# Halved first products and a seeded last accumulation in a retention + two-MLP kernel

## The chip, the core and the metric

The kernel runs on one core of one Trainium2 chip. The metric is the device time of one execution in microseconds (us). Before the change it is 582.34 us, the median of two runs (582.31 and 582.37).

## What is computed

A retention layer (linear attention with a per-head decay, 2 batches of 8 heads, 768 positions of 64 channels) gives a matrix x of 1536 tokens by 512 channels. Two MLPs follow. Everything is in float32.

```python
h = x @ w_in                                        # first MLP: 512 -> 2048
g = np.maximum(h, 0.0) + alpha * np.minimum(h, 0.0)
x = g @ w_out                                       # 2048 -> 512
h = x @ w_in2                                       # second MLP
r = np.maximum(h, 0.0)
out = (r * r) @ w_out2
```

## The kernel before, in words

Retention comes first (up to line 538, about the first 54 us). The change touches only the second MLP, and there only its last part.

Both MLPs work on token tiles of 512 tokens (`TT`, three tiles t = 0, 1, 2) and on 16 blocks f of 128 hidden channels (`NF`). To keep float32 accuracy each operand is split into a high and a low part of type fp32r (`wh`, `wl`, `xh`, `xl`, `gh`, `gl`), and each product is three matmuls: low times high, high times low, high times high.

A **step** is one pair (t, f) of one MLP m. The list `STEPS` (line 47) has 96 of them, 48 for each MLP, in the order of `PARTS` (lines 34 to 38). A **part** is a run of blocks f of one token tile that is accumulated in PSUM without interruption. The second MLP's parts are tile 0 with f 0 to 7, tile 1 with f 0 to 7, tile 2 with all f, tile 1 with f 8 to 15, and last tile 0 with f 8 to 15. These last eight are the steps 88 to 95; tile 1's second part before them is steps 80 to 87.

For each step s the loop at line 553 does:

1. `first` (line 169): 12 matmuls of 512 columns into one PSUM bank (4 blocks of the 512 input channels, 3 matmuls each), line 176. The innermost loop takes the weights in the order wl, wh, wh.
2. `activate` (line 181): for the second MLP a Relu on ScalarE (line 185), the square as a multiplication on VectorE (line 186), and the rounding to `gh` on ScalarE (line 195).
3. `rest` (line 198): `gl` on VectorE (line 200).
4. `load_sums` (line 235), at the last step of a part that continues an earlier one: four DMAs of 256 KB, issued by SyncE (line 238), fetch the earlier part's sums from DRAM into four tiles `ps` of the pool `pp`.
5. `second` (line 203) of step s - 2 (`LAG` is 2): for each of four groups i, three matmuls of 512 columns into the accumulator `acc[t][i]` (lines 226 to 231; 12 in all, line 231 in the second MLP). The accumulators rotate over PSUM banks 3 to 7. In the last part, the products of f = 14 are held back and done together with those of f = 15, group by group.

At the end of a part `end_sum` (line 240) empties each accumulator. A first part is copied to a tile `p` by ScalarE (line 250) and written to DRAM as sums (line 252). A part that continues one is added to `ps` by VectorE (line 245), and the result goes to the output by a DMA on SyncE's queue (line 255).

Every engine runs its own instructions in the order in which the program issues them, and waits at an instruction for what that needs. SyncE's queue too: its DMAs start in the program's order. The pool `pp` (line 85) has four buffers for all `p` and `ps` tiles, so a new `ps` tile waits until the DMA has read the tile that had the buffer before:

```python
    pp = ctx.enter_context(tc.tile_pool(name="pp", bufs=4))
...
        p_of[t] = [pp.tile([128, 512], F32, tag="p", name=f"ps{m}_{t}_{i}") for i in range(4)]
        for i in range(4):
            nc.sync.dma_start(p_of[t][i], sums[m, t, i])
```

Of the kernel before, what the change touches and what calls it, by code (L numbers as in the profile page):

```python
# [21 lines left out]
NC = DM // 128  # L22
NF = DFF // 128
TT = 512
# [9 lines left out]
PARTS = [  # L34
    [(0, range(4)), (1, range(4)), (2, range(8)), (1, range(4, 8)), (0, range(4, 16)),
     (1, range(8, 16)), (2, range(8, 16))],
    [(0, range(8)), (1, range(8)), (2, range(16)), (1, range(8, 16)), (0, range(8, 16))],
]
LAG = 2
# [12 lines left out]
    if 0 <= i < len(STEPS)  # L52
]
SEQ = list(dict.fromkeys(USES))
BACC = dict(dynamic_dma_scratch_size=4096)


@with_exitstack
def retention_then_two_mlps(
# [15 lines left out]
    nc = tc.nc  # L75
# [17 lines left out]
    def bank(name, banks):  # L93

        i = used[banks] = used.get(banks, -1) + 1
        return psum["mlp"].tile([128, 512], F32, tag=f"bank{banks[i % len(banks)]}", name=name)
# [13 lines left out]
    def load_piece(queue=nc.scalar):  # L110
        if len(loaded) < 4 * NF:
            j = SEQ[len(loaded)]
            loaded.append(j)
# [4 lines left out]
    class Conversion:  # L118
# [3 lines left out]
        def start(self, k):  # L122
            if k < 4 * NF and SEQ[k] not in bits:
                j = SEQ[k]
                low, high = raws[j][:, :, 0], raws[j][:, :, 1]
                bits[j] = x = bitp.tile([128, DM], U32, tag="bits", name=f"bits{j}")
                nc.scalar.activation(x.bitcast(F32), high.bitcast(F32), AF.Copy, scale=REBIAS)  # L127
                nc.scalar.activation(low.bitcast(I32), low, AF.Copy, scale=2.0**-29)  # L128

        def begin(self):  # L130

            j = SEQ[self.k]
            x, high = bits[j], raws[j][:, :, 1]
# [5 lines left out]
        def middle(self, load=True):  # L139

            j = SEQ[self.k]
            x, low, slot = bits[j], raws.pop(j)[:, :, 0], j % (2 * NF)
# [7 lines left out]
        def end(self):  # L150
            j = SEQ[self.k]
            x, hi, slot = bits.pop(j).bitcast(F32), weights[j], j % (2 * NF)
            lo = wpools[slot // 2].tile([128, DM], F32R, tag=f"wl{slot}", name=f"wl{j}")
            nc.vector.tensor_tensor(lo, x, hi.bitcast(F32), ALU.subtract)  # L154
            weights[j] = hi, lo
            self.k += 1
# [7 lines left out]
    steps = STEPS  # L164
    x_of = {(0, t): xt[t] for t in range(NTILE)}
    g_of, acc = {}, {}
    sums = dram.tile([2, NTILE, 4, 128, TT], F32, name="sums")

    def first(m, t, f):
        wh, wl = weights[2 * (m * NF + f)]  # L170
        xh, xl = x_of[m, t]
        ph = bank(f"h{m}_{t}_{f}", (0, 1, 2))
        for c in range(NC):
            cols = slice(c * 128, (c + 1) * 128)
            for i, (w, x) in enumerate(((wl, xh), (wh, xl), (wh, xh))):
                nc.tensor.matmul(  # L176
                    ph, w[:, cols], x[:, c, :], start=c == 0 and i == 0, stop=c == NC - 1 and i == 2
                )
        return ph

    def activate(m, t, f, ph, on_act):
        g = tp.tile([128, TT], F32, tag="g", name=f"g{m}_{t}_{f}")
        a = alpha_sb[:, f : f + 1]
        if m == 1:
            nc.scalar.activation(g, ph, AF.Relu)  # L185
            nc.vector.scalar_tensor_tensor(g, ph, 0.0, g, ALU.max, ALU.mult)  # L186
        elif on_act:
            nc.scalar.activation(g, ph, AF.Relu, scale=-1.0)
            nc.scalar.activation(g, g, AF.Copy, scale=a)  # L189
            nc.vector.scalar_tensor_tensor(g, ph, 0.0, g, ALU.max, ALU.subtract)  # L190
        else:
            nc.vector.tensor_scalar(g, ph, 0.0, a, ALU.min, ALU.mult)
            nc.vector.scalar_tensor_tensor(g, ph, 0.0, g, ALU.max, ALU.add)
        gh = gp.tile([128, TT], F32R, tag="gh", name=f"gh{m}_{t}_{f}")
        nc.scalar.copy(gh, g)  # L195
        return g, gh

    def rest(m, t, f, g, gh):
        gl = gp.tile([128, TT], F32R, tag="gl", name=f"gl{m}_{t}_{f}")
        nc.vector.tensor_tensor(gl, g, gh.bitcast(F32), ALU.subtract)  # L200
        g_of[m, t, f] = gh, gl

    def second(m, t, f, part):
        if f == part[0]:
            acc[t] = [bank(f"acc{m}_{t}_{f}_{i}", (3, 4, 5, 6, 7)) for i in range(4)]

        last = m == 1 and (t, part) == PARTS[1][-1]
        if last and f == NF - 2:
            return
        fs = (NF - 2, NF - 1) if last and f == NF - 1 else (f,)  # L210
        for i in range(4):
            for e in fs:
                partial_sum(m, t, e, part, i)
            if f == part[-1]:
                end_sum(m, t, part, i)
        for e in fs:
            g_of.pop((m, t, e))
        if m == 0 and f == NF - 1:
            next_x(t, part)

    def partial_sum(m, t, f, part, i):
        wh, wl = weights[2 * (m * NF + f) + 1]
        gh, gl = g_of[m, t, f]
        cols = slice(i * 128, (i + 1) * 128)

        for j, (w, g) in enumerate(((wl, gh), (wh, gh), (wh, gl))):
            flags = dict(start=f == part[0] and j == 0, stop=f == part[-1] and j == 2)
            if m == 0:
                nc.tensor.matmul(acc[t][i], w[:, cols], g, **flags)  # L229
            else:  # L230
                nc.tensor.matmul(acc[t][i], g[:, cols], w, **flags)  # L231

    p_of = {}

    def load_sums(m, t):
# [4 lines that stand above are left out]
    def end_sum(m, t, part, i):  # L240

        done = part[-1] == NF - 1
        if part[0] > 0:
            p = p_of[t][i]
            nc.vector.tensor_tensor(p, acc[t][i], p, ALU.add)  # L245
        elif m == 0 and done:
            p = acc[t][i]
        else:
            p = pp.tile([128, 512], F32, tag="p", name=f"p{m}_{t}_{part[0]}_{i}")
            nc.scalar.copy(p, acc[t][i])  # L250
        if not done:
            nc.sync.dma_start(sums[m, t, i], p)
        elif m == 1:
            c, b = ORDER[t * CPT + i]
            nc.sync.dma_start(out[b * S + c * CH : b * S + (c + 1) * CH, :], p)
        else:
            acc[t][i] = p

    def next_x(t, part):
        xh, xl = x_of[1, t] = x_tile("xb", t)  # L260
        ps = acc.pop(t)
        for i in range(5):
            if i < 4:
                nc.scalar.copy(xh[:, i, :], ps[i])
            if i > 0:
                nc.vector.tensor_tensor(
                    xl[:, i - 1, :], ps[i - 1], xh.bitcast(F32)[:, i - 1, :], ALU.subtract
                )
# [51 lines left out]
    def where(name, shape, pattern, base, fill, channel=1):  # L320

        x = ap1.tile(shape, F32, name=name)
        zeros = warm[0 : shape[0], 0 : shape[-1]]
        if len(shape) == 3:
            zeros = zeros.unsqueeze(1).to_broadcast(shape)
        nc.gpsimd.affine_select(
            x, zeros, pattern=pattern, compare_op=ALU.not_equal, fill=fill, base=base,
            channel_multiplier=channel,
        )
        return x  # L330

    head = ap1.tile([H, NPAIR, 2, D], F32, name="head")
    for t in range(2):
        m = where(f"head{t}", [H, NPAIR, D], [[-2, NPAIR], [0, D]], -t, 1.0)
# [218 lines left out]
    for s in range(len(steps) + LAG):  # L553
        if s < len(steps):
            m, t, f, part = steps[s]
            sums_end = s >= LAG and steps[s - LAG][2] == steps[s - LAG][3][-1]
            unit = conv.k < 4 * NF and not sums_end
            if unit and SEQ[conv.k] >= 2 * NF and free[(SEQ[conv.k] - 2 * NF) // 2] >= s:
                unit = False
            if unit:  # L560
                conv.start(conv.k + 1)
                conv.begin()
            ph = first(m, t, f)
            g, gh = activate(m, t, f, ph, unit)
            if unit:
                conv.middle()
            rest(m, t, f, g, gh)
            if unit:
                conv.end()
            if f == part[-1] and part[0] > 0:  # L570
                load_sums(m, t)
        if s >= LAG:
            second(*steps[s - LAG])


# [58 lines left out]
```

## Time and profile before

| | us |
|---|---|
| time, median of 2 runs | 582.34 |
| the profiled execution | 582.9 |
| its span, first to last instruction | 580.6 |
| TensorE (PE) busy | 572.1 |
| weight loads (PEld) busy | 475.7 |
| VectorE (DVE) busy | 334.7 |
| ScalarE (ACT) busy | 293.6 |
| mean granted TensorE clock (1.0 is full) | 1.00 |

The profile is of one execution. Times in its rows are counted from the span's start. A matmul's duration in a row includes its way through the array and so overlaps with the next one's; the distance from start to start says how fast matmuls follow each other. "L176" is line 176. "SPq" is SyncE's queue of DMA issues, "PEld" the weight load that belongs to a matmul.

### The profile page before, as it was taken

What the parts mean: (1) busy time and instruction counts of PE and PEld (TensorE: products, weight loads), DVE (VectorE), ACT (ScalarE), POOL (GpSimd) and SP (SyncE); (2) the same over time, 40 slices, a digit from 0 to 9 for tenths busy, and PEclk for the clock granted to TensorE, in tenths of its full rate; (3) what the DMA queues carried; (4) which work ended last, traced back from release to release, by engine and by line L of the source; (5) the groups of instructions that cost most, each with busy time, mean ns of one, the idle gap of its engine ahead of it and who ended that gap; (6) DMA issues with size and microseconds to landing.
All of it is one profiled execution on the core that took longest, in us unless ns stands there. A gap on an engine that the chain in (4) does not pass through costs nothing.

```text
span 580.6 us, 7855 instructions
## 1 busy us (share of the span) xinstructions
PE 572.1 (99%) x3058; PEld 475.7 (82%) x3058; DVE 334.7 (58%) x535; ACT 293.6 (51%) x509; POOL 33.3 (6%) x34
## 2 busy tenths in 40 slices
PE   8998999999999999999999999999999999999997
PEld 7887888888888888888888888888888888888885
DVE  3888766666666666866866965665632222222422
ACT  2566765765746765765765654654522222322220
POOL 2785000000000000000000000000000000000000
PEclk9999999999999999999999999999999999999999
DMA  7993343323544223333333123423100000400401
GB/s 255 361 393 120 108 146 109 117 102 109 192 147 168 82 100 109 110 108 110 108 110 109 51 94 110 141 78 109 73 0 1 0 1 0 146 0 1 145 2 72
DMA packets 25732, 62.38 MB, mean 107 GB/s; under 512 B 2904, under 2 KB 3936, under 8 KB 25696
## 3 DMA queue, kind: packets, MB, share of 16 engines
q1 hardware_dynamic: 17488, 32.01, 15.7%
q10 hardware_dynamic: 8208, 29.89, 15.5%
q8 instruction: 24, 0.39, 0.3%
q14 instruction: 12, 0.10, 0.0%
HBM read 52.44 MB, written 9.45 MB: 107 GB/s over the span
## 4 chain that ended last, share of the span: by engine, by line
PE 95%; DMA 3%; DVE 1%; issue 0%; SPq 0%; DVEq 0%
PE h L176 45%; PE acc L231 22%; PE acc L229 22%; PE o L436 2%; PE o L444 2%; PE s L399 1%; DMA q<-in_qt_dram 1%; DMA r<-in_kr_dram 1%; DMA zd<-z 1%; PE pk L459 1%; DMA lam_sb<-in_lam_dram 0%; DVE err L358 0%; DVE ps L245 0%; SPq L304 0%; DVE low L359 0%
## 5 line engine op out<-in xcount | busy, mean ns | idle before, releaser
L195 ACT CAST gh<-g 128x512 fp32r<-128x512 f32 x96 | 59.6, 621 | 90.5 <-DVE g L186 37.5
L186 DVE SCALAR_TENSOR_TENSOR g<-h,g 128x512 f32<-128x512 f32 x48 | 33.2, 691 | 123.4 <-ACT g L185 123.4
L185 ACT ACTIVATE g<-h 128x512 f32<-128x512 f32 x48 | 28.7, 598 | 124.3 <-PE h L176 124.3
L200 DVE TENSOR_TENSOR gl<-g,gh 128x512 fp32r<-128x512 f32 x96 | 66.5, 692 | 30.3 <-ACT gh L195 21.6
L176 PE MATMUL h<-xah,wl 128*128 128x512 f32 x192 | 74.8, 390 | 0.0
L176 PE MATMUL h<-xah,wh 128*128 128x512 f32 x192 | 74.7, 389 | 0.0
L176 PE MATMUL h<-xal,wh 128*128 128x512 f32 x192 | 74.7, 389 | 0.0
L229 PE MATMUL acc<-gh,wl 128*128 128x512 f32 x192 | 74.7, 389 | 0.0
L229 PE MATMUL acc<-gh,wh 128*128 128x512 f32 x192 | 74.7, 389 | 0.0
L229 PE MATMUL acc<-gl,wh 128*128 128x512 f32 x192 | 74.7, 389 | 0.0
L176 PE MATMUL h<-xbh,wl 128*128 128x512 f32 x192 | 74.7, 389 | 0.0
L176 PE MATMUL h<-xbl,wh 128*128 128x512 f32 x192 | 74.7, 389 | 0.0
L176 PE MATMUL h<-xbh,wh 128*128 128x512 f32 x192 | 74.7, 389 | 0.0
L231 PE MATMUL acc<-wl,gh 128*128 128x512 f32 x192 | 74.7, 389 | 0.0
L231 PE MATMUL acc<-wh,gh 128*128 128x512 f32 x192 | 74.7, 389 | 0.0
L231 PE MATMUL acc<-wh,gl 128*128 128x512 f32 x192 | 74.7, 389 | 0.0
L190 DVE SCALAR_TENSOR_TENSOR g<-h,g 128x512 f32<-128x512 f32 x42 | 29.0, 691 | 62.2 <-ACT g L189 62.2
L135 DVE SCALAR_TENSOR_TENSOR bits<-raw,bits 128x512 uint32<-128x512 uint32 x64 | 46.9, 733 | 2.2
L154 DVE TENSOR_TENSOR wl<-bits,wh 128x512 fp32r<-128x512 f32 x64 | 44.6, 697 | 2.7 <-ACT wh L145 2.7
L143 DVE CUSTOM_DVE_ANT_0 bits<-raw,bits 128x1024 uint16<-128x1024 uint16 x64 | 46.0, 718 | 0.0
L127 ACT ACTIVATE bits<-raw 128x512 f32<-128x512 f32 x64 | 43.0, 672 | 0.7 <-DMA raw<-in_w_dram 0.6
L128 ACT ACTIVATE raw<-raw 128x512 int32<-128x512 uint32 x64 | 42.7, 667 | 0.0
(73 smaller groups left out, 786.4 us busy)
## 6 DMA issues: line engine op xcount, KB each, us to landing
raw<-in_w_dram ACTq DMA_DIRECT2D x57, 512.0 KB, 3.3
ps<-sums SPq DMA_DIRECT2D x24, 256.0 KB, 3.1
sums<-p SPq DMA_DIRECT2D x20, 256.0 KB, 2.2
raw<-in_w_dram SPq DMA_DIRECT2D x7, 512.0 KB, 6.3
k<-in_kt_dram SPq DMA_DIRECT2D x12, 256.0 KB, 5.9
q<-in_qt_dram SPq DMA_DIRECT2D x12, 256.0 KB, 5.3
v<-in_vr_dram SPq DMA_DIRECT2D x12, 256.0 KB, 6.0
r<-in_kr_dram SPq DMA_DIRECT2D x10, 256.0 KB, 5.7
```

The source lines that it names most:

```text
L127: nc.scalar.activation(x.bitcast(F32), high.bitcast(F32), AF.Copy, scale=REBIAS)
L128: nc.scalar.activation(low.bitcast(I32), low, AF.Copy, scale=2.0**-29)
L135: nc.vector.scalar_tensor_tensor(x, high, 0x80000000, x, ALU.bitwise_and, ALU.bitwise_or)
L143: nc.vector.tensor_tensor(x.bitcast(I32), x.bitcast(I32), low.bitcast(I32), ALU.add)
L154: nc.vector.tensor_tensor(lo, x, hi.bitcast(F32), ALU.subtract)
L176: nc.tensor.matmul(ph, w[:, cols], x[:, c, :], start=c == 0 and i == 0, stop=c == NC - 1 and i == 2)
L186: nc.vector.scalar_tensor_tensor(g, ph, 0.0, g, ALU.max, ALU.mult)
L190: nc.vector.scalar_tensor_tensor(g, ph, 0.0, g, ALU.max, ALU.subtract)
L195: nc.scalar.copy(gh, g)
L200: nc.vector.tensor_tensor(gl, g, gh.bitcast(F32), ALU.subtract)
L229: nc.tensor.matmul(acc[t][i], w[:, cols], g, **flags)
L231: nc.tensor.matmul(acc[t][i], g[:, cols], w, **flags)
```

## The change

Two edits. The first products of steps 88 to 91 (second MLP, tile 0, f 8 to 11) are issued as 24 matmuls of 256 columns in place of 12 of 512: each pair of halves has the same weights and writes the two halves of the same bank. And the last part (steps 88 to 95) is seeded: at its start ScalarE copies the four `ps` tiles into the four accumulators, the matmuls then add to them, and at the end the accumulator is copied to a tile `p` by ScalarE (line 250 of before) where VectorE had added `ps`. The loads of the sums for this part are issued in step 89, after `second` of step 87, where they were issued in step 95.

```diff
@@ -52,6 +52,7 @@
+HALVED = range(8, 12)
@@ -170,12 +171,17 @@ first
         ph = bank(f"h{m}_{t}_{f}", (0, 1, 2))
+        cut = TT // 2 if (m, t) == (1, 0) and f in HALVED else TT
+        halves = [slice(a, a + cut) for a in range(0, TT, cut)]
         for c in range(NC):
             cols = slice(c * 128, (c + 1) * 128)
             for i, (w, x) in enumerate(((wl, xh), (wh, xl), (wh, xh))):
-                nc.tensor.matmul(
-                    ph, w[:, cols], x[:, c, :], start=c == 0 and i == 0, stop=c == NC - 1 and i == 2
-                )
+                for ts in halves:
+                    nc.tensor.matmul(
+                        ph[:, ts], w[:, cols], x[:, c, ts],
+                        start=c == 0 and i == 0 and ts.start == 0,
+                        stop=c == NC - 1 and i == 2, skip_group_check=len(halves) > 1,
+                    )
         return ph
@@ -200,9 +206,15 @@
+    def seeded(m, t, part):
+        return m == 1 and (t, part) == PARTS[1][-1]
+
     def second(m, t, f, part):
         if f == part[0]:
             acc[t] = [bank(f"acc{m}_{t}_{f}_{i}", (3, 4, 5, 6, 7)) for i in range(4)]
+            if seeded(m, t, part):
+                for i in range(4):
+                    nc.scalar.copy(acc[t][i], p_of[t][i])
@@ -224,7 +236,10 @@ partial_sum
-            flags = dict(start=f == part[0] and j == 0, stop=f == part[-1] and j == 2)
+            flags = dict(
+                start=f == part[0] and j == 0 and not seeded(m, t, part),
+                stop=f == part[-1] and j == 2, skip_group_check=seeded(m, t, part),
+            )
@@ -240,7 +255,7 @@ end_sum
-        if part[0] > 0:
+        if part[0] > 0 and not seeded(m, t, part):
             p = p_of[t][i]
             nc.vector.tensor_tensor(p, acc[t][i], p, ALU.add)
@@ -567,10 +582,14 @@ main loop
-            if f == part[-1] and part[0] > 0:
+            if f == part[-1] and part[0] > 0 and not seeded(m, t, part):
                 load_sums(m, t)
         if s >= LAG:
             second(*steps[s - LAG])
+        if LAG <= s < len(steps) and seeded(*steps[s][:2], steps[s][3]):
+            m, t, f, part = steps[s]
+            if f == part[0] + 1:
+                load_sums(m, t)
```

## Rows read from the trace of the kernel before

**Rows 1.** The page: span, busy time of the engines, chain by engine.
```profile
span 580.6 us, 7855 instructions
PE 572.1 (99%) x3058; PEld 475.7 (82%) x3058; DVE 334.7 (58%) x535; ACT 293.6 (51%) x509; POOL 33.3 (6%) x34
PE 95%; DMA 3%; DVE 1%; issue 0%; SPq 0%; DVEq 0%
```
**Rows 2.** Chain that ended last, 530 to 581 us: start, us, what.
```profile
541.51 2.72 PE acc L231 x12
...
568.71 8.17 PE acc L231 x36
...
576.91 0.69 DVE ps L245
```
**Rows 3.** Timeline of PE, 538 to 545 us (start, duration): step 90.
```profile
538.63 0.39 PE L176 MATMUL h<-xbh,wl 128*128 128x512 f32 x1
538.86 0.39 PE L176 MATMUL h<-xbl,wh 128*128 128x512 f32 x1
...
541.35 0.39 PE L231 MATMUL acc<-wl,gh 128*128 128x512 f32 x1
...
544.07 0.39 PE L176 MATMUL h<-xbh,wl 128*128 128x512 f32 x1
```
**Rows 4.** Timeline of the other engines, 535 to 552 us (idle time before in brackets).
```profile
538.73 2.48 DVE L245 TENSOR_TENSOR ps<-acc,ps 128x512 f32<-128x512 f32 x4
539.44 2.13 SPq L255 DMA_DIRECT2D out_dram<-ps  x4
541.55 0.60 ACT L185 ACTIVATE g<-h 128x512 f32<-128x512 f32 x1 [3.46 <-PE h L176]
541.66 2.51 SPq L238 DMA_DIRECT2D ps<-sums  x4
542.90 0.62 ACT L195 CAST gh<-g 128x512 fp32r<-128x512 f32 x1 [0.76 <-DVE g L186]
```
**Rows 5.** Line 238 in 533 to 549 us: issues, and time to landing.
```profile
L238 SPq DMA_DIRECT2D ps<-sums x4: 319/333/404, 541.7 to 543.9; - x4
DMA to landing us min/median/max: 3.0/3.2/3.4
```
**Rows 6.** DMA traffic, 539 to 548 us in 40 slices of 0.225 us.
```profile
GB/s 0 0 0 0 0 91 400 364 392 401 364 382 382 373 401 355 382 218 164 137 264 400 364 382 364 373 246 282 273 346 337 237 228 182 127 100 9 0 0 0
```
**Rows 7.** Groups by line and form: busy us, mean ns, idle before.
```profile
L176 PEld LDWEIGHTS h<-xbh,wh 128*128 128x128 f32 x192 | 36.1, 188 | 7.4
L176 PEld LDWEIGHTS h<-xbl,wh 128*128 128x128 f32 x192 | 36.0, 188 | 7.6
L436 PE MATMUL o<-sc,v 128*64 128x128 f32 x192 | 13.1, 279 | 1.9 <-issue 1.6 <-PE o L436 0.3
L250 ACT COPY p<-acc 128x512 f32<-128x512 f32 x24 | 12.2, 595 | 0.0
```
**Rows 8.** Timelines of PE and PEld, 13 to 15.2 us: the second warm-up.
```profile
13.08 2.05 PE L318 MATMUL warm_ps<-warm 128*128 128x128 f32 x16
...
13.08 1.86 PEld L318 LDWEIGHTS warm_ps<-warm 128*128 128x128 f32 x16
```
**Rows 9.** Line 318, durations min/median/max, and PE's timeline; a stretch (PE busy, clock, DMA).
```profile
L318 PE MATMUL warm_ps<-warm x40: 275/275/580, 1.0 to 14.9; 128*128 128x128 f32 x40
...
0.99 4.45 PE L318 MATMUL warm_ps<-warm 128*128 128x128 f32 x24 [0.99 <-POOL warm L313]
...
0.90:1.50 0.60, 0.51 (x2) 1.00 0.00 0
```
**Rows 10.** PE's timeline, 44 to 62 us; the stretch 46 to 52 us.
```profile
50.25 1.09 PE L436 MATMUL o<-sc,v 128*64 128x128 f32 x16 [1.58 <-issue]
...
46.00:52.00 6.00, 4.42 (x79) 1.00 0.30 95
```
**Rows 11.** Line 245, durations min/median/max, all 24.
```profile
L245 DVE TENSOR_TENSOR ps<-acc,ps x24: 681/681/692, 169.0 to 576.9; 128x512 f32<-128x512 f32 x24
```

## The prediction

> **What bounds the kernel now.** I read the page first: TensorE is busy for 572.1 of 580.6 us, and the chain that ended last lies on it for 95% [rows 1]. The chain in order of time then shows where this holds around the change: products follow products, 2.72 us for every twelve, without a gap, until the last product, one VectorE addition and the output DMA [rows 2]. So in the steps concerned each microsecond in which TensorE stands still is a microsecond of the time, and other engines' work is worth nothing except after the last product. The timeline of TensorE gives the unit: twelve first products start from 538.63 to 541.35, so one matmul of 512 columns takes 0.227 us from start to start, and a group of three 0.68 us [rows 3]. These are step 90's, and the products from 541.35 to 544.07 are `second` of step 88: the first that would need a seed. The timeline of the other engines shows where the sums are then [rows 4]: their loads are issued only at 541.66 us, after TensorE has begun those products. Before, nothing needs them until the end of the part, 30 us later.
>
> **Halves.** Four steps issue 24 matmuls for 12, and 24 weight loads for 12: `first` uses wh twice in a row already, and each of these has its own load (192 loads with xbl and 192 with xbh, 188 ns each) [rows 7], so equal weights are not skipped. No row has 256 columns with these weights. The nearest is the second warm-up, 128 columns behind a load of 128: 15 distances in 2.05 less 0.275 us, 0.118 us each [rows 8, 9]. These are held by their loads, for retention's products of 128 columns behind loads of 64 come at (1.09 - 0.28) / 15 = 0.054 us [rows 10, 7]. So 512 columns alone would take 0.216 us, and 0.011 of the 0.227 belongs to each matmul; 256 columns by the same sum take 0.108 + 0.011, some 0.120 us. A step then takes 24 x 0.120 = 2.88 us, 0.16 more than 2.72, and that is what I take, since the warm-up's 0.118 lies right beside it. The lower end is columns alone, 24 x 0.108 = 2.59 us, 0.13 less. A straight line through 0.118 and 0.227 would give 0.154 us and 0.98 more for a step; the upper end is a load of 0.188 us that nothing overlaps, 24 x 0.188 = 4.51 us, 1.79 more.
>
> The Trainium skill ("TensorE: Matmul & The Clock Gate", Back-to-back issue gap) gives N/2.4 + 2.5 ns from one matmul to the next at the full clock. For 512 columns that is 216 ns, where the rows have 227; by it a halved step would cost 24 x 0.109 less 12 x 0.216, only 0.03 us more, and the four steps 0.1 in place of 0.6. I go by the row.
>
> **The loads of the sums.** They move six steps up in the program, from step 95 to 89, but on SyncE's queue nothing lies between: the four output DMAs of step 87's part (539.44 on) come first in either order, and the loads right behind them. They wait there for buffers, since the pool has four and the outputs still hold them: the first load starts at 541.66, 2.2 us after the first output, the last at 541.66 + 2.51 - 0.32 = 543.85 [rows 4, 5]. So the move itself brings the loads forward by nothing. They land 3.0 to 3.4 us after their issue [rows 5]: the first at 544.7; the last about 547.2, where the traffic ends (slice 37, 547.1 to 547.3) [rows 6].
>
> **The seeds.** Four copies on ScalarE, ahead of `second` of step 88. In its queue they stand behind step 90's Relu and rounding to `gh`, which waits for VectorE's square in between, and which ends at 542.90 + 0.62 = 543.52 [rows 4]. A copy of this size from PSUM takes 0.595 us, the rounding 0.62 [rows 7, 4]; none in the trace writes PSUM, so I take 0.595 and keep 0.4 to 0.62. Behind the waiting copies stands step 91's Relu, which TensorE can't feed before it has passed the seeds, so nobody else waits.
>
> Now the times, with the halves: steps 88 and 89 push everything by 0.32 us, since the outputs follow `end_sum`, and this VectorE's work of step 89. TensorE reaches the seeded products at 541.35 + 3 x 0.16 = 541.83. `gh` is done by 544.0. The first sum lands at 545.0, its copy ends at 545.6: TensorE restarts at 545.65, after 3.8 us. The last sum lands at 547.5; with 0.05 us for the hand-overs its copy ends at 548.15. Three groups from 545.65 would be done at 547.7, so this last landing decides, and the fourth group's 0.68 us ends the phase at 548.85. Before it ended at 544.07: 4.8 us lost, in which step 90's own 0.16 is hidden. Step 91's halves add 0.16. After that the sequence is as before, later by the sum.
>
> **The end.** VectorE's additions of 0.681 us [rows 11] become copies of 0.595 us on ScalarE, which has nothing else to do there. Three of the four lie beside later products; the last is on the path and saves 0.09 us (bounds: a saving of 0.06 to 0.2). The output DMA behind it stays.
>
> **Sum.** 4.8 + 0.16 - 0.09 = 4.9 us. The profiled execution took 582.9 us, its span and 2.3 us around it, and would become 587.8; it lies 0.56 us above the median of the runs, which becomes 587.2 us. Ends: all sums land in 3.0 us and copies take 0.4, 0.6 less; halves at half of 0.227 us, 0.5 less, by columns alone 0.4 less again, and by the straight line 2.5 more (the last landing 1.64 later, step 91 0.82). Without anything from the rivals that is 585.7 to 589.7.
>
> **Rivals.**
>
> *The clock falls in the gap.* TensorE will stand idle for about 3.7 us and then work in short groups until 548.9. The longest gap of this trace is 1.58 us (ahead of 50.25), and the granted clock of the stretch is 1.00 [rows 10]; a longer one it doesn't have. What coming back from the lower level (1.2 GHz) costs is seen at the start, where TensorE came from rest: 23 distances in 4.45 - 0.275 = 4.18 us, against 23 x 0.118 = 2.71 us, though the granted clock is shown as 1.00 there; durations reach 580 ns for 275 [rows 8, 9]. That is 1.5 us lost: 588.7 us, and up to twice that if the groups' pauses draw it out, 590.1. Chance 15%: the gap is longer than any seen, but twice that of one that did nothing.
>
> The Trainium skill ("TensorE: Matmul & The Clock Gate", Part 1: The HAM clock gate) says that an idle TensorE drops to half its clock and has to be busy for a while before it is given the full one back. The slow first warm-up agrees with the second half of that; no row here shows the first half.
>
> *The weight loads bound the halves.* If a load of 0.188 us can't overlap the halves, each halved step takes 1.79 us more. The last sum lands 3.58 us later than before, at 550.8; its group ends at 552.1, 8.0 us late; with step 91's 1.79 and the end the total is +9.7 us, 592.0. For it speaks only the duration of the load [rows 7]; against it, the warm-up's loads have the same duration and follow each other at 0.118 us [rows 8]. Chance 6%.
>
> *Not slower: the seeds come in time.* Then only the end counts, 582.34 - 0.09 = 582.25 us, if the halves also go at half of 0.227 us, or 582.9 with them at 0.120. The place is the wait for the first seed: it would have to be copied by 541.83, so its load would have to land by 541.2 and be issued by 538.2, and the last by 540.2. For it: the loads are asked for a whole step ahead in the program. Against it: the buffers are held by outputs that are not even computed until 538.73 [rows 4]. It holds only if the new order gives the loads other buffers or a way past the outputs, and I see neither. Chance 4%.
>
> That the loads were late before and come earlier by their new place is excluded by the same row: they are issued as soon as the first buffer is free already.
>
> **How the numbers follow.** Forecast 75%, clock 15%, weight loads 6%, not slower 4%. The time is that of the forecast, 587.2 us; its low end 585.6 takes in the bounds of halves, copies and landings, and the high end 590.4 the straight line, and the clock with its doubling. The loads' case and the one that is not slower are left out, with 10% together. Two per cent, about what a measurement of this kernel can tell from no change, is 11.6 us: all cases but a sum of the two bad ones (over 594.0 us) lie within. Faster by over 2% 1%, within 2% 97%, slower by over 2% 2%.
>
> **What would show it.** TensorE's idle time, none in this stretch before, has one gap of about 3.8 us ahead of the first product of `second` of step 88, released by a ScalarE copy which itself waited for the DMA of the sums; two or three short ones follow within 3 us. The loads' issues lie 0.3 us later than before, not earlier. The halved matmuls start 0.120 us apart. At the end a ScalarE copy stands in the place of VectorE's addition. I am wrong if the gap is under 2 us (the loads got ahead of the outputs), if the copies wait for something other than the DMA, or if matmuls behind the gap start 0.43 us apart (clock).

## The result, and the profile after

The changed kernel takes 588.71 us, the median of two runs (588.44 and 588.98), against 582.34 before: a ratio of 1.0109 with the 95% interval 1.0066 to 1.0153. It is slower, by 6.4 us where 4.9 were forecast; the time lies in the predicted range, 585.6 to 590.4. In a further comparison with more rounds it was 589.23 us against 582.02, 1.012 (1.0101 to 1.0138).

The page of the changed kernel: span, busy time, chain by engine, to be read beside [rows 1].

```profile
span 586.4 us, 7955 instructions
...
PE 575.8 (98%) x3106; PEld 480.4 (82%) x3106; DVE 331.8 (57%) x531; ACT 298.2 (51%) x517; POOL 33.2 (6%) x34
...
PE 93%; DMA 4%; DVE 1%; issue 0%; ACT 0%; SPq 0%; DVEq 0%
```

The span is 5.8 us longer, and TensorE, which now has 48 matmuls more, is busy for only 3.7 us more; the rest is time in which it stands still. The timeline of TensorE shows where, to be read beside [rows 3].

```profile
527.20 0.40 PE L180 MATMUL h<-xbh,wl 128*128 128x256 f32 x2
...
538.44 0.40 PE L180 MATMUL h<-xbh,wl 128*128 128x256 f32 x2
...
541.07 0.40 PE L180 MATMUL h<-xbh,wh 128*128 128x256 f32 x2
545.17 0.50 PE L246 MATMUL acc<-wl,gh 128*128 128x512 f32 x1 [3.71 <-ACT acc L217]
...
546.22 0.49 PE L246 MATMUL acc<-wh,gh 128*128 128x512 f32 x1
546.51 0.63 PE L246 MATMUL acc<-wh,gl 128*128 128x512 f32 x1
547.18 0.80 PE L246 MATMUL acc<-wl,gh 128*128 128x512 f32 x1
547.78 0.63 PE L246 MATMUL acc<-wh,gh 128*128 128x512 f32 x1
548.21 0.63 PE L246 MATMUL acc<-wh,gl 128*128 128x512 f32 x1
...
549.86 0.40 PE L180 MATMUL h<-xbh,wl 128*128 128x256 f32 x2
...
552.74 0.40 PE L246 MATMUL acc<-wl,gh 128*128 128x512 f32 x1
```

One pair of halves follows another after 0.239 us (538.44 to 541.07 for eleven), so 0.120 us for a half. After step 90's first products TensorE stands still for 3.71 us until ScalarE has copied the first seed (line 217). And the last products before step 91's first ones at 549.86 are 0.43 us apart (547.78 to 548.21) where they were 0.227. The windows of TensorE say what that is; the columns are the stretch, busy time and instructions, the granted clock, the DMA share and GB/s.

```profile
545.00:546.00 1.00, 0.82 (x4) 1.00 0.96 311
546.00:547.00 1.00, 1.00 (x4) 0.69 0.28 107
...
548.00:549.00 1.00, 1.00 (x3) 0.50 0.00 0
549.00:550.00 1.00, 1.00 (x5) 0.61 0.00 0
550.00:551.00 1.00, 1.00 (x11) 1.00 0.00 0
```

The granted clock goes to 0.50, the lower of its two levels (1.2 GHz), between 546 and 547: a mean of 0.69 in that microsecond puts the fall at 546.4, during the fifth product behind the standstill. It is back at 1.00 by 550, after TensorE has worked almost without a pause since 547.18. This is the rival "the clock falls in the gap".

Who made TensorE wait is in the timeline of the other engines, to be read beside [rows 4],

```profile
539.22 2.12 SPq L270 DMA_DIRECT2D out_dram<-ps  x4
541.44 2.48 SPq L253 DMA_DIRECT2D ps<-sums  x4
...
542.86 0.62 ACT L201 CAST gh<-g 128x512 fp32r<-128x512 f32 x1 [0.76 <-DVE g L192]
...
544.53 1.30 ACT L217 COPY acc<-ps 128x512 f32<-128x512 f32 x2 [1.06 <-DMA ps<-sums]
546.54 1.26 ACT L217 COPY acc<-ps 128x512 f32<-128x512 f32 x2 [0.71 <-DMA ps<-sums]
```

and in the chain that ended last, which no longer keeps to TensorE here.

```profile
540.41 2.25 DMA out_dram<-ps
...
542.72 3.80 DMA ps<-sums
```

An output holds a buffer, the load (the third of the four) waits for it, the copy waits for the load, the products wait for the copy. ScalarE's copies wait for the DMA twice; `gh` was long done.

The account goes by the distances within each profile. From step 88's first product to the first one behind its second products it is 549.86 - 527.20 = 22.66 us, and in the kernel before, whose step 88 begins at

```profile
527.75 0.39 PE L176 MATMUL h<-xbh,wl 128*128 128x512 f32 x1
```

it is 544.07 - 527.75 = 16.32: 6.34 more. Of these the halves of steps 88 to 90 are 0.5. At the full clock the last two groups would have taken from 547.18 to 548.54 instead of 549.86: 1.3 for the clock. The remaining 4.5 are the wait. Step 91's halves add 0.16, and the end gives back 0.15. The changed kernel's profile came to step 88 0.55 us earlier, without any change ahead of it; so the spans differ by 5.8. Such differences are usual here: 15 runs of the kernel before lay between 580.85 and 582.63 us.

### The profile page after: what moved, and what is told of

Same layout as the page of the kernel before. It is cut to its first block, busy times and chain, and to the rows that moved or that the text cites. A ratio compares the mean times of both kernels' runs of the same rounds, so it can differ in the third digit from the quotient of the medians.

```text
span 586.4 us, 7955 instructions
## 1 busy us (share of the span) xinstructions
PE 575.8 (98%) x3106; PEld 480.4 (82%) x3106; DVE 331.8 (57%) x531; ACT 298.2 (51%) x517; POOL 33.2 (6%) x34
## 4 chain that ended last, share of the span: by engine, by line
PE 93%; DMA 4%; DVE 1%; issue 0%; ACT 0%; SPq 0%; DVEq 0%
PE h L180 44%; PE acc L244 22%; PE acc L246 22%; PE o L451 2%; PE o L459 2%; PE s L414 1%; DMA q<-in_qt_dram 1%; PE pk L474 1%; DMA r<-in_kr_dram 1%; DMA zd<-z 1%; DMA ps<-sums 1%; DMA out_dram<-ps 0%; DVE ps L260 0%; DMA lam_sb<-in_lam_dram 0%; DVE err L373 0%
## 5 line engine op out<-in xcount | busy, mean ns | idle before, releaser
L180 PE MATMUL h<-xbl,wh 128*128 128x512 f32 (+1 forms) x208 | 75.0, 373 | 0.0
L180 PE MATMUL h<-xbh,wl 128*128 128x512 f32 (+1 forms) x208 | 75.0, 373 | 0.0
L180 PE MATMUL h<-xbh,wh 128*128 128x512 f32 (+1 forms) x208 | 75.0, 373 | 0.0
L246 PEld LDWEIGHTS acc<-wl,gh 128*128 128x128 f32 x192 | 36.3, 189 | 12.2 <-ACT acc L217 4.9
L180 PEld LDWEIGHTS h<-xbh,wl 128*128 128x128 f32 x208 | 38.5, 189 | 7.2
```

Source lines behind the costliest of these rows:

```text
L180: nc.tensor.matmul(ph[:, ts], w[:, cols], x[:, c, ts], start=c == 0 and i == 0 and ts.start == 0, stop=c == NC - 1 and i == 2, skip_group_ ...
```

## The experiments

All edits are to the changed kernel, except where said otherwise. The first four were compared with one another on one chip, beside 15 runs of the kernel before (582.02 us).

**The changed kernel again.** No edit.

> The changed kernel, timed in more rounds. Theory (the wait for the seeds costs 4.5 us, and the clock falls behind it for some 3 us and costs another 1.3): 588.4 to 589.0 us, and granted clock 0.5 behind the gap in the profile. Rival (the clock falls only in some executions): times in two groups, near 587.4 and near 588.7.

Measured 589.23 us, 1.012 (1.0101 to 1.0138). In its profile the clock is low for longer than in the first; windows of TensorE:

```profile
544.00:545.00 1.00, 0.11 (x1) 0.59 0.95 338
...
551.00:552.00 1.00, 1.00 (x11) 0.99 0.00 0
```

Here it fell while TensorE still stood still, and was low for nearly 7 us in place of some 3.4. So the price of the clock differs from one execution to the next. The four executions took 589.22, 589.43, 589.24 and 587.48 us. The last lies where the rival puts an execution in which the clock holds, and the record doesn't decide whether it held: its mean granted clock is 0.997, as in the first profile, in which the clock fell, but executions of the kernel before have 0.996 to 1.000 as well. The rival is left open for this one.

**Seeds without halves.**

```diff
-HALVED = range(8, 12)
+HALVED = range(0)
```

> The seeds without the halves. Theory: the loads of the sums come 0.32 us earlier (two halved steps fewer before them), step 91 is 0.16 us shorter, and step 90's halves were hidden in the wait: 0.5 us less than the changed kernel, 588.2 us, with a gap of 3.9 us in place of 3.7 and the clock at 0.5 behind it. Rival (the halves are what brings the clock near its fall, by a weaker load of TensorE before the gap): the clock holds and the time is 586.9 us.

587.99 us, 1.0103 (1.0087 to 1.0118). The theory's 588.2 was reckoned from 588.7; beside the changed kernel of the same comparison it is 1.2 us less where 0.5 was expected, and the two intervals overlap. The gap is longer by 0.17 us, and behind it the products are at half speed from the first on; TensorE's timeline:

```profile
544.26 0.80 PE L246 MATMUL acc<-wl,gh 128*128 128x512 f32 x1 [3.88 <-ACT acc L217]
544.86 0.63 PE L246 MATMUL acc<-wh,gh 128*128 128x512 f32 x1
```

So the clock falls without the halves too, and the rival is out.

**Halves without seeds.**

```diff
     def seeded(m, t, part):
-        return m == 1 and (t, part) == PARTS[1][-1]
+        return False
```

> The halves without the seeds. Theory: 4 x 0.16 = 0.64 us more than before, 583.0 us, matmuls 0.120 us apart. Rival (halves cost nothing where no wait follows): 582.3 us.

583.09 us, 1.002 (1.0011 to 1.0028). That is 1.1 us more than the kernel before beside it, where 0.64 was expected; the interval, 0.6 to 1.6 us, is too wide to tell a step's price. The trace is finer: a step of the halved stretch takes 5.61 us, 0.17 over 5.44 (twice 2.72):

```profile
526.32 0.40 PE L180 MATMUL h<-xbh,wl 128*128 128x256 f32 x2
...
529.19 0.40 PE L246 MATMUL acc<-wl,gh 128*128 128x512 f32 x1
529.42 0.40 PE L246 MATMUL acc<-wh,gh 128*128 128x512 f32 x1
529.66 0.39 PE L246 MATMUL acc<-wh,gl 128*128 128x512 f32 x1
...
531.93 0.40 PE L180 MATMUL h<-xbh,wl 128*128 128x256 f32 x2
```

The halves themselves take 2.87 us; the remaining 0.02 us are in the products behind them, of which the first few are 0.23 to 0.24 us apart.

**The gap filled.** Fifteen products that nothing reads, ahead of the seeded ones.

```diff
         if s >= LAG:
+            if steps[s - LAG] == (1, 0, 8, PARTS[1][-1][1]):
+                idle = bank("idle", (0, 1, 2))
+                wh, xh = weights[2 * (NF + 10)][0], x_of[1, 0][0]
+                for k in range(15):
+                    nc.tensor.matmul(idle, wh[:, 0:128], xh[:, k % NC, :], start=True, stop=True)
             second(*steps[s - LAG])
```

> The changed kernel with 15 products of 512 columns that nothing reads, put into the gap ahead of the seeded products (3.4 us of the 3.9). Theory (the gap lets the clock fall): granted clock 1.00 throughout, products behind the gap 0.227 us apart, 1.3 us less than the changed kernel, 587.4 us, although it computes more. Rival (the products behind the gap are slow because they add onto banks that ScalarE has just written, or beside its copies): they stay 0.43 us apart and the time stays at 588.7 us.

587.16 us, 1.0087 (1.0071 to 1.0102): 2.1 us less than the changed kernel beside it, though it computes more. TensorE's timeline, and its windows behind the gap:

```profile
541.63 3.59 PE L592 MATMUL idle<-xbh,wh 128*128 128x512 f32 x15
545.47 0.50 PE L246 MATMUL acc<-wl,gh 128*128 128x512 f32 x1 [0.25 <-ACT acc L217]
545.80 0.39 PE L246 MATMUL acc<-wh,gh 128*128 128x512 f32 x1
546.03 0.40 PE L246 MATMUL acc<-wh,gl 128*128 128x512 f32 x1
...
547.59 0.50 PE L246 MATMUL acc<-wl,gh 128*128 128x512 f32 x1 [0.46 <-ACT acc L217]
```

```profile
546.00:547.00 1.00, 1.00 (x5) 1.00 0.67 254
```

The seeds come no earlier, and the products behind them run beside ScalarE's copies and add onto banks that ScalarE has just written, as before; but they are 0.23 us apart, at a clock of 1.00. This settles it: the slow products were the clock's, and the clock fell for want of work. The rival is out.

The next four had 23 runs of the kernel before beside them (582.15 us).

**Step 91's first products ahead of the seeded ones.**

```diff
+    ahead = {}
...
-            ph = first(m, t, f)
+            ph = ahead.pop(s, None) or first(m, t, f)
...
         if s >= LAG:
+            if steps[s - LAG] == (1, 0, 8, PARTS[1][-1][1]):
+                ahead[s + 1] = first(*steps[s + 1][:3])
             second(*steps[s - LAG])
```

> The changed kernel, with step 91's first products (2.9 us) issued ahead of the seeded products instead of behind them. Theory (TensorE only waits there, and what it does in the gap is free): 2.9 us less for the products and about 2 for the clock, which holds since the gap shrinks to some 0.9 us: 584.3 us beside a changed kernel at 589.2. Rival (the copies are held up by whatever stands before them on ScalarE and slide with the order): the gap reopens behind step 91's products and the time stays above 587 us.

584.11 us, 1.0031 (1.002 to 1.0042), 0.2 from the theory. The gap shrinks to 0.93 us, with one of 0.32 behind it, and the clock stays at 1.00:

```profile
545.20 0.50 PE L246 MATMUL acc<-wl,gh 128*128 128x512 f32 x1 [0.93 <-ACT acc L217]
...
547.20 0.50 PE L246 MATMUL acc<-wl,gh 128*128 128x512 f32 x1 [0.32 <-ACT acc L217]
```

The first seed is used at 545.20, as in the changed kernel (545.17): the copies don't slide. Useful work in the gap is worth its own length and the clock's price.

**Other buffers for the sums, same place in the program.** The sums go into the staging buffers of the weights, free by then.

```diff
-        p_of[t] = [pp.tile([128, 512], F32, tag="p", name=f"ps{m}_{t}_{i}") for i in range(4)]
+        if m == 1 and t == 0:
+            raw = [rawp.tile([128, DM, 2], U32, tag="raw", name=f"ps{m}_{t}_{i}") for i in range(2)]
+            raw = [r.rearrange("p a b -> p (a b)").bitcast(F32) for r in raw]
+            p_of[t] = [raw[i // 2][:, i % 2 * 512 : (i % 2 + 1) * 512] for i in range(4)]
+        else:
+            p_of[t] = [...]
```

> The changed kernel, with the last part's sums loaded into the staging buffers of the weights, which nobody uses by then, at the same place in the program. Theory A (the loads are held by the outputs' place on SyncE's queue as much as by the buffers): they are issued from 541.4 us on at 0.45 us from one to the next, share the DMA engines with the outputs, and the last lands about 0.9 us earlier; the gap stays near 3.5 us, the clock falls still: 588.3 us. Theory B (the buffers alone hold them): the gap goes, 583 us.

588.70 us, 1.0109 (1.0088 to 1.013). SyncE's issues of the loads and the first seeded product:

```profile
541.38 1.95 SPq L258 DMA_DIRECT2D ps<-sums  x4
```

```profile
545.48 0.80 PE L246 MATMUL acc<-wl,gh 128*128 128x512 f32 x1 [4.03 <-ACT acc L217]
```

Four issues in 1.95 us where there were 2.48: the buffers held only the later loads, the last of them by 0.7 us (issued at 542.9 where it was 543.6). The first is issued at 541.38 where it was 541.44, so the outputs' place on the queue holds it as much as the buffers did. Theory A, but for the gap, which is longer (4.0 us), not shorter: the first load lands 3.4 us after its issue, where it took 3.1 in the changed kernel, and the first sum comes later for it. That the outputs still on their way slow the load is argued, not shown.

**The same, with the loads ahead of the outputs on the queue.**

```diff
+        if LAG <= s < len(steps) and seeded(*steps[s][:2], steps[s][3]):
+            m, t, f, part = steps[s]
+            if f == part[0]:
+                load_sums(m, t)
         if s >= LAG:
             second(*steps[s - LAG])
-        if LAG <= s < len(steps) and seeded(*steps[s][:2], steps[s][3]):
...
```

> As own_buffers, with the loads asked for one step earlier in the program, ahead of the outputs on SyncE's queue. Theory: the sums lie ready many us early; now the copies wait for ScalarE, behind step 90's rounding to gh, which ends 2.2 us after TensorE is through with step 90; first copy done 2.8 us after that: a gap of 2.8 us, four copies back to back end before their groups, so 2.8 us lost in all: 585.4 us with the clock held, 587 if it falls. Rival (the DMA was the only thing waited for): 582.7 us.

587.50 us, 1.01 (1.0076 to 1.0124): 587 was expected if the clock falls. The first of the last part's loads on SyncE, then step 90's `gh` and the copies on ScalarE, then TensorE's first seeded product and the window behind its gap:

```profile
L258 SPq DMA_DIRECT2D ps<-sums x1: 422/422/422, 499.4 to 499.4; - x1
```

```profile
542.84 0.62 ACT L201 CAST gh<-g 128x512 fp32r<-128x512 f32 x1 [0.76 <-DVE g L192]
543.36 2.14 ACT L217 COPY acc<-ps 128x512 f32<-128x512 f32 x4
```

```profile
544.00 0.80 PE L246 MATMUL acc<-wl,gh 128*128 128x512 f32 x1 [2.55 <-ACT acc L217]
```

```profile
544.00:545.00 1.00, 1.00 (x2) 0.50 0.00 0
```

The loads are issued from 499.4 us on, 42 us early. Now the copies follow step 90's `gh` at once, without a wait for a DMA. So there are two waits, one behind the other: the DMA, and ScalarE's queue; taking away the first alone leaves 2.55 us. And 2.55 us of standing still are enough for the clock to fall. The six executions fall into two groups: four of 586.90 to 587.83 us, each with a mean granted clock of 0.997, and two of 589.33 and 590.48 us with 0.991. Those two lie 2.2 and 3.4 us above the median of the four.

**The copies ahead of step 90's Relu as well.**

```diff
             ph = first(m, t, f)
+            if seeded(m, t, part) and f == part[0] + LAG:
+                seeds = [bank(f"acc{m}_{t}_{part[0]}_{i}", (3, 4, 5, 6, 7)) for i in range(4)]
+                for i in range(4):
+                    nc.scalar.copy(seeds[i], p_of[t][i])
             g, gh = activate(m, t, f, ph, unit)
...
```

(`second` then takes these banks in place of making and filling its own.)

> As own_early, with the four copies put ahead of step 90's Relu on ScalarE's queue. Theory: no wait is left; the halves' 0.7 us more and 0.1 less at the end, 582.6 us beside 582.0 of before, no gap of TensorE, clock 1.00. Rival (the copies then wait for VectorE to empty the accumulators of the part before, and push step 90's Relu): a gap of up to 1 us ahead of the seeded products, 583.6 us.

582.67 us, 1.0006 (0.9994 to 1.0018): the wait is gone and the clock is 1.00 through the stretch. What is left, 0.5 us, fits the halves' price but can't be told from nothing. TensorE's first seeded product, now without idle time before it, and the window around it:

```profile
542.45 0.40 PE L248 MATMUL acc<-wl,gh 128*128 128x512 f32 x1
```

```profile
542.00:543.00 1.00, 1.00 (x9) 1.00 1.02 375
```

ScalarE's copies wait for VectorE, as the rival says, but early enough:

```profile
538.92 0.58 ACT L589 COPY acc<-ps 128x512 f32<-128x512 f32 x1
540.37 1.79 ACT L589 COPY acc<-ps 128x512 f32<-128x512 f32 x3 [0.87 <-DVE ps L267]
542.71 0.60 ACT L191 ACTIVATE g<-h 128x512 f32<-128x512 f32 x1 [0.55 <-PE h L180]
```

**Early seeds without halves**, that is, with `HALVED = range(0)` besides; the last two kernels had 15 runs of the kernel before beside them (582.09 us).

> The early seeds without the halves. Theory: nothing is left but the end, where a copy of 0.59 us stands for an addition of 0.68: 0.1 us less than before, too little to be told from it, TensorE without a gap. Rival (the seeding itself costs TensorE something, since its first products add onto a bank that another engine wrote): 0.5 us or more over before.

582.00 us, 0.9999 (0.9989 to 1.0008). Seeding itself costs TensorE nothing that can be measured, and gains nothing either: no version here is faster than the kernel before.

**All 48 steps of the second MLP in halves**, no seeds.

```diff
-        cut = TT // 2 if (m, t) == (1, 0) and f in HALVED else TT
+        cut = TT // 2 if m == 1 else TT
...
     def seeded(m, t, part):
-        return m == 1 and (t, part) == PARTS[1][-1]
+        return False
```

> No seeds, and the first products of all 48 steps of the second MLP in halves. Theory A (0.177 us for a step, of which 0.16 in the halves and 0.02 in the products that follow them): 8.5 us more than before, 590.6 us beside 582.1. Theory B (0.16 us a step, the rest was an accident of one profile): 7.7 us more, 589.8. Rival (in a long row the weight loads fall behind and bound the halves): over 600 us.

590.95 us, 1.0153 (1.0139 to 1.0167): 8.9 us more, 0.185 us for a step; in the trace a step takes 2.87 + 2.75 = 5.62 us, 0.18 over 5.44. Theory B is out, theory A is 0.4 us short, and the weight loads don't fall behind in a long row.

This profile shows something else of the clock. It falls early in retention, some 530 us before the stretch of this case. The longest standstill between TensorE's first product and this fall is 0.51 us:

```profile
11.10 1.71 PE L414 MATMUL s<-q,k 64*128 64x128 f32 x16 [0.51 <-DMA q<-in_qt_dram]
```

```profile
11.00:12.00 1.00, 0.90 (x12) 0.77 0.83 246
12.00:13.00 1.00, 1.00 (x12) 0.50 1.06 268
```

In the profile of the kernel before, the same stretch has standstills of 0.75 and 0.63 us, and the clock stays at 1.00. So one long standstill is enough for the clock to fall, but it is not needed; what else makes it fall was not tried.

## Why the prediction was right or wrong

The sign, the place and the mechanism of the wait were right, and the range held the time. The likeliest case, given 75%, was not the one that happened: it said 587.2 with the clock held, and the kernel with the clock held by filler products takes 587.16 beside 582.02, 5.1 more where 4.9 were forecast. What happened is the first rival, given 15%, and one of the prediction's own signs of being wrong, products 0.43 us apart behind the gap, came true. The range held the time because its high end took in this rival. That the rival's 588.7 is met to the tenth is luck: the wait and the halves cost 0.2 us more than forecast, the clock in that profile 0.2 less, and the same kernel timed again takes 589.23.

- **Halves: right.** 0.120 us each, as summed from columns and a rest for each matmul; the straight line (0.154) and the load that nothing overlaps (0.188) are out. A step costs 0.17 to 0.185 us, not 0.16: the products behind the halves are slowed a little too, which the forecast didn't have. By the rule of the Trainium skill ("TensorE: Matmul & The Clock Gate", Back-to-back issue gap) 256 columns would take an estimated 109 ns; the trace has 120.
- **The loads of the sums: right in what mattered.** Their new place brings them forward by nothing: counted from step 88's first product they are issued after 14.24 us, before after 13.91. That the four buffers are the reason was only half of it: with other buffers the first load is issued at the same time, held by the outputs ahead of it on the queue.
- **The wait: right.** At the full clock the phase would have lost 5.0 us, 4.5 of wait and 0.5 of halves, where 4.8 were forecast. The gap was to be 3.8 us; between the products' starts, as the forecast counts, it is 3.86 (541.31 to 545.17). The forecast let the last landing decide. It was the third: that load landed 3.80 us after its issue, more than the 3.0 to 3.4 read before, and the fourth right behind it. The end of the phase moved by little.
- **The clock: the step that failed.** "The gap is longer than any seen, but twice that of one that did nothing" was taken for a sign that the clock would hold. One gap of 1.58 us says nothing about 3.7. In all five profiles with a gap of 2.55 to 4.03 us at this place the clock fell; in the two with 0.46 us and 0.93 us at most it held. That an idle TensorE drops to half its clock (the Trainium skill, "TensorE: Matmul & The Clock Gate", Part 1: The HAM clock gate) is now shown by rows of this case: in the second profile of the changed kernel the clock goes to 0.50 before the standstill ends. The price, read from the slow first warm-up as 1.5 us and up to twice that, was about right: 1.3 in the first profile, 2.1 between the medians with and without filler.
- **The end: right.** A copy of 0.58 us in the place of the addition of 0.68:

```profile
582.88 0.58 ACT L265 COPY p<-acc 128x512 f32<-128x512 f32 x1 [0.77 <-PE acc L246]
```

- **The other rivals.** The weight loads don't bind. "The seeds come in time" is not this change; the runs that end without a wait have three things together, added one after the other: other buffers, a place ahead of the outputs on SyncE's queue, and one ahead of Relu on ScalarE's. Whether fewer would do was not tried.

## What to carry to other kernels

An addition at the end of an accumulation, beside other work, costs only its last piece (here 0.09 us over a copy); the same data as a seed is needed at the beginning, and then everything in front of it in a buffer, a DMA queue and an engine's queue is on the path. Before moving a consumer earlier, list what its data waits for, one queue after the other, since taking one wait away brings up the next. And where the bounding engine is TensorE, price a standstill of a few microseconds with the clock: its length, plus what the low clock costs behind it (here 1.3 to 2.1 us, and more in single executions), or fill it with work that is needed anyway.

## What the runs showed of the hardware

A standstill of 2.55 us was enough for the granted clock to go to 0.50; those of 0.93 us and 1.58 us left it at 1.00; and once, in retention, it fell after no standstill over 0.51 us since TensorE's first product. When it falls varies: within the standstill in one execution, during the fifth product behind it in another; so does the time for which it stays low, some 3.4 us in one profile and nearly 7 us in another of the same kernel. Products behind a halved step are a little slower for the first few, up to 0.24 us apart instead of 0.227; why was not tried.
